# Second pieces of the first four attention units: the values' products from split parts in two passes, in place of float32

## The chip, the core and the metric

The kernel runs on one core of a Trainium2 chip. The engines are TensorE (PE in the profile, with its weight loads as PEld), VectorE (DVE), ScalarE (ACT), GpSimd (POOL) and SyncE (SP), which here issues every DMA. The metric is the device time in microseconds (us) of one execution, and a kernel's time is the median of its runs.

## The reference

Three layers follow one another, and every one takes and gives float32:

```python
# attention: B, H, S, D = 4, 8, 576, 64
scores = scale * q @ k^T ; causal mask ; a = softmax(scores)
local  = a @ v                                   # the products that the change touches
mem    = (phi(q) @ M_prev) / (phi(q) @ z_prev + 1e-6)
x      = g * mem + (1 - g) * local               # as 2304 x 512
# first layer: 512 -> 2048 -> 512, silu;  second layer: 512 -> 1024 -> 512, softmax times h, layer norm
```

## The kernel before

**Units.** The 32 pairs of batch and head are worked off as 16 units of two heads each, so four units make one batch. The first four units (`u < NN`, `NN = 4`) are cut into a first piece (queries 0 to 256) and a second piece (queries 256 to 576); units 4 to 15 are done whole. Each such piece is a *turn*; sorted by place, the first pieces are turns 0 to 3, the second pieces turns 4 to 7.

**A turn** runs over tiles of 128 queries. For one tile, TensorE makes the scores (`pss`), VectorE adds the mask and takes the maximum (`a`, `nm`), ScalarE takes the exponential, TensorE transposes the result in blocks of 128 (`pst`), and the blocks are copied out of PSUM into a wide tile `aT` (`t_hi`, `t_lo`). When all tiles of a head are there, `av` multiplies the values with `aT` (`psav`) and the sum goes into `xs`. `finish` scales it and adds the memory term into `X` on GpSimd.

**Two ways to multiply.** For the units below `NN` the values `rawv` and the tile `aT` are float32, and a product is one call, which shows in the trace as two matmul records. The tiles `aTh` and `aTl` are then two buffers of that one kind, and turns take them by turns (`turn_of[u] % 2`); the values alternate too, between the buffers `rawv` and `vhl`. For the other units everything is split in two parts that TensorE takes in one pass each: `aTh` is the rounded part (made by ScalarE) and `aTl` the rest (a subtraction on VectorE), `vhl` holds the rounded values (a cast on VectorE) beside their rest (a subtraction on GpSimd); a product is then two matmuls into one accumulator, one with `aTh` and one with `aTl`, and both halves of the accumulator are added (a copy on ScalarE and an addition on VectorE).

**The fill.** Between the turns TensorE works on the first layer of batches whose `X` is ready (`psh`, `psfy`). While the second pieces run there is only the fill of batch 0, columns 0 to 256: 72 matmuls `psh` and 72 `psfy`. The next, columns 256 to 576, needs all four second pieces. The weights `w` for it are split once on the way (`wraw` to `wf` to `w`), three VectorE instructions for each half chunk.

**The order** is not that of the source. Every call gets a due time (`call`, `at`), and a planner (`Order.plan`) goes through a model of the five engines: it takes the operation that can start first, then the one due first, as far as buffers are free, and writes the operations down in that sequence. Each engine then works its own queue in order. Nearly all instructions are issued by one line of this class, which the profile calls L360, so tiles' names tell them apart.

The lines that decide which way a unit goes:

```python
n = ("f", turn_of[u] % 2) if u < NN else ("r", n)                       # a_of
if u < NN: v_t[u] = raw.rearrange("p c j d -> p c (j d)"); return        # split_v, cut
for to, ps in t_pairs(u, t) if u >= NN else ():                          # t_lo
```

Of the kernel before, what the change touches and what calls it, by code (L numbers as in the profile page):

```python
# [11 lines left out]
F32 = mybir.dt.float32  # L12
F32R = mybir.dt.float32r
# [22 lines left out]
NN = 4  # L36
# [327 lines left out]
def body(ctx, tc, qk, qk2, qt, vp, mz, beta, w1, w2i, w2o, gln, out):  # L364
# [150 lines left out]
    st = {}  # L515
    heads, raws, v_t, mem_t, s_t, unit, X, Xd, Yd = {}, {}, {}, {}, {}, {}, {}, {}, {}
    a_t = {}

    def a_of(u, n=0):


        n = ("f", turn_of[u] % 2) if u < NN else ("r", n)
        if n not in a_t:
            a_t[n] = p1.tile([128, 3840], F32 if u < NN else F32R, tag=f"aT{n[1]}", name="aT" + "hl"[n[1]])

            act.copy(heads_of(a_t[n])[64:128, :, 1024:1088], tri[64:128, 0:128].rearrange("p (j q) -> p j q", j=2))
        return a_t[n]


# [46 lines left out]

    def load_v(u, q1):
        n = (q1 + 127) // 128
        st["v"] = st.get("v", 0) + (u < NN)
        raws["v", u] = p1.tile([128, 5, 2, 64], F32, tag="vhl" if u < NN and st["v"] % 2 else "rawv", name="rawv")[:, 0:n]  # L580
        sp.dma_start(raws["v", u], vp[u, :, 0:n].rearrange("p c (j d) -> p c j d", j=2))

    def split_v(u, q1):
        raw = raws.pop(("v", u))
        if u < NN:
            v_t[u] = raw.rearrange("p c j d -> p c (j d)")
            return
        vhl = p1.tile([128, 5, 2, 128], F32R, tag="vhl", name="vhl")[:, 0:(q1 + 127) // 128]
        dve.tensor_copy(vhl[:, :, :, 0:64], raw)
        pool.tensor_tensor(vhl[:, :, :, 64:128], raw, f32(vhl[:, :, :, 0:64]), ALU.subtract)  # L590
        v_t[u] = vhl
# [155 lines left out]
    def heads_of(w):  # L747
        return w[:, 0:3840].rearrange("p (j c) -> p j c", j=2)
# [20 lines left out]
    def t_hi(u, t, n):  # L769
        turn_of[u] = n  # L770
        for to, ps in t_pairs(u, t):
            if u < NN and t > 4:
                dve.tensor_copy(to(a_of(u)), ps)
            else:
                act.copy(to(a_of(u)), ps)

    def t_lo(u, t):
        for to, ps in t_pairs(u, t) if u >= NN else ():
            dve.tensor_tensor(to(a_of(u, 1)), ps, f32(to(a_of(u))), ALU.subtract)
        s_t.pop((u, t))  # L780

    def av(u, j, segs, last):
        vhl = v_t[u]
        if ("s", u) not in unit:
            unit["s", u] = p2.tile([128, S], F32, tag="xs", name="xs")
        xs = unit["s", u]
        to, other = (UP, LOW) if j == 0 else (LOW, UP)
        for q0, q1 in segs:
            ps = ps_a.tile([128, q1 - q0], F32, tag="av", name="psav")
            kbs = [kb for kb in range(5) if 128 * kb < q1]  # L790
            for kb in kbs:
                f = max(q0, 128 * kb)
                w = a_cols(j, kb, f, q1)
                if u < NN:
                    pe.matmul(ps[:, f - q0:], vhl[:, kb], a_of(u)[:, w], start=(kb == 0), stop=(kb == kbs[-1]))
                    continue
                pe.matmul(ps[:, f - q0:], vhl[:, kb, j, :], a_of(u)[:, w], start=(kb == 0), stop=False)
                pe.matmul(ps[:, f - q0:], vhl[:, kb, j, :], a_of(u, 1)[:, w], start=False, stop=(kb == kbs[-1]))
            if u < NN:
                act.copy(xs[to, q0:q1], ps[to])  # L800
                continue
            act.copy(xs[to, q0:q1], ps[other])
            dve.tensor_tensor(xs[to, q0:q1], ps[to], xs[to, q0:q1], ALU.add)
        if last:
            v_t.pop(u)
# [365 lines left out]
```

## Time and profile before

| | before |
|---|---|
| three runs | 925.24, 929.64, 929.32 us |
| median | 929.32 us |
| the profiled execution: its own time | 926.01 us |
| its span, first to last instruction | 923.2 us |
| PE busy | 880.5 us (95%) |
| DVE busy | 593.7 us (64%) |
| ACT busy | 495.8 us (54%) |
| POOL busy | 401.8 us (44%) |

The profiled execution took 926.01 us, of which 2.8 us lie around the span; it is 3.3 us below the median. Busy time is the union of an engine's instructions, and matmul ends are modelled, so neighbouring matmuls overlap in the rows: how long a row of them takes is read from start to start, not from the durations. Starts are counted from the begin of the span.

### The profile page before, as it was taken

What the parts mean: (1) busy time and instruction counts of PE and PEld (TensorE: products, weight loads), DVE (VectorE), ACT (ScalarE), POOL (GpSimd) and SP (SyncE); (2) the same over time, 40 slices, a digit from 0 to 9 for tenths busy, and PEclk for the clock granted to TensorE, in tenths of its full rate; (3) what the DMA queues carried; (4) which work ended last, traced back from release to release, by engine and by line L of the source; (5) the groups of instructions that cost most, each with busy time, mean ns of one, the idle gap of its engine ahead of it and who ended that gap; (6) DMA issues with size and microseconds to landing.
All of it is one profiled execution on the core that took longest, in us unless ns stands there. A gap on an engine that the chain in (4) does not pass through costs nothing.

```text
span 923.2 us, 15757 instructions
## 1 busy us (share of the span) xinstructions
PE 880.5 (95%) x5762; PEld 801.8 (87%) x5762; DVE 593.7 (64%) x1396; ACT 495.8 (54%) x1201; POOL 401.8 (44%) x334
## 2 busy tenths in 40 slices
PE   8989999999999999999889998899899999999998
PEld 6666899998899999998889998799889888888886
DVE  4777779878777757157984228832656666666663
ACT  5767689878787867455553335434443333232222
POOL 4555588877767653334542225423533111111110
PEclk9999999999999999999999999999999999999999
DMA  6525243343323210453342003300000000000000
GB/s 214 167 86 174 89 158 109 123 142 100 108 88 102 89 42 1 184 227 124 115 136 92 1 1 114 111 5 1 1 1 2 12 23 23 24 23 24 23 24 34
DMA packets 26653, 71.97 MB, mean 78 GB/s; under 512 B 3152, under 2 KB 10064, under 8 KB 25680
## 3 DMA queue, kind: packets, MB, share of 16 engines
q1 hardware_dynamic: 26576, 70.97, 23.3%
q8 instruction: 45, 0.74, 0.3%
q14 instruction: 32, 0.26, 0.1%
HBM read 60.34 MB, written 10.62 MB: 77 GB/s over the span
## 4 chain that ended last, share of the span: by engine, by line
PE 68%; DVE 18%; ACT 6%; issue 4%; DMA 3%; POOL 0%; ACTq 0%; DVEq 0%; SPq 0%
PE psh L360 24%; PE pso L360 11%; PE psy L360 11%; DVE wf L360 9%; PE pst L360 5%; PE psav L360 5%; PE pss L360 5%; PE psfy L360 5%; DMA wraw<-in_w 2%; DVE phe L360 2%; DVE a L360 1%; DVE aTl L360 1%; PE psr L360 1%; ACT wf L360 1%; PE psm L360 1%
## 5 line engine op out<-in xcount | busy, mean ns | idle before, releaser
L360 PE MATMUL psh<-xh,w 128*128 128x288 f32 (+2 forms) x1024 | 205.4, 300 | 1.7 <-ACT w L360 1.7
L360 PEld LDWEIGHTS psh<-xh,w 128*128 128x128 f32 x1024 | 161.5, 189 | 4.0 <-ACT w L360 1.9
L360 POOL TENSOR_TENSOR xl<-x,xh 128x1152 fp32r<-128x1152 f32 (+3 forms) x35 | 88.1, 2520 | 117.7 <-ACT xh L360 108.1
L360 PE MATMUL psh<-xl,w 128*128 128x288 f32 (+2 forms) x512 | 137.2, 299 | 0.0
L360 DVE TENSOR_TENSOR glo<-psh,gh 128x288 fp32r<-128x288 f32 (+2 forms) x128 | 57.7, 452 | 120.3 <-ACT gh L360 120.2
L360 PE MATMUL psy<-gh,w 128*128 128x288 f32 x736 | 117.1, 297 | 7.4 <-DVE y L360 4.1
L360 PEld LDWEIGHTS psy<-gh,w 128*128 128x128 f32 x736 | 104.2, 188 | 10.5 <-ACT gh L360 5.4
L360 POOL TENSOR_TENSOR w<-wf,w 128x512 fp32r<-128x512 f32 x48 | 65.8, 1372 | 103.4 <-ACT w L360 103.3
L360 PE MATMUL pso<-w,tb 128*128 128x512 f32 x432 | 104.0, 397 | 0.0
L360 ACT ACTIVATE a<-a,nm 128x128 f32<-128x128 f32 (+4 forms) x144 | 84.5, 588 | 23.2 <-DVE nm L360 21.9
L360 PEld LDWEIGHTS pso<-w,tb 128*128 128x128 f32 x432 | 79.9, 188 | 17.2
L360 PEld LDWEIGHTS psh<-xl,w 128*128 128x128 f32 x512 | 91.7, 190 | 0.1
L360 PE MATMUL psh<-w,yh 128*128 128x512 f32 x288 | 90.2, 394 | 0.0
L360 DVE SCALAR_TENSOR_TENSOR wf<-wraw,wf 128x512 uint32<-128x512 uint32 x96 | 86.7, 903 | 3.1
L360 DVE CUSTOM_DVE_ANT_0 a<-pss,tri 128x128 f32<-128x128 f32 (+4 forms) x144 | 67.6, 476 | 21.3 <-PE pss L360 17.4
L360 PE MATMUL psy<-glo,w 128*128 128x288 f32 x368 | 68.3, 301 | 12.2 <-DVE glo L360 12.1
L360 PE MATMUL pst<-ident,a 128*128 128x128 f32 (+1 forms) x400 | 70.2, 280 | 5.0 <-ACT rb L360 2.1
L360 ACT ACTIVATE psh<-psh 128x288 f32<-128x288 f32 x84 | 33.1, 395 | 72.0 <-PE psh L360 71.9
L360 DVE TENSOR_TENSOR aTl<-pst,aTh 128x128 fp32r<-128x128 f32 (+3 forms) x120 | 56.2, 484 | 18.6 <-ACT aTh L360 18.2
L360 PEld LDWEIGHTS psy<-glo,w 128*128 128x128 f32 x368 | 55.5, 191 | 14.0 <-DVE glo L360 14.0
L360 PE MATMUL psfy<-gh,w 128*128 128x288 f32 (+2 forms) x288 | 63.6, 303 | 1.8 <-ACT w L360 1.7
L360 PEld LDWEIGHTS psh<-w,yh 128*128 128x128 f32 x288 | 53.9, 188 | 11.9
(129 smaller groups left out, 1900.3 us busy)
## 6 DMA issues: line engine op xcount, KB each, us to landing
wraw<-in_w SPq DMA_DIRECT2D x32, 512.0 KB, 3.8
rawqk<-in_qk SPq DMA_DIRECT2D x24, 608.0 KB, 3.9
rawv<-in_vp SPq DMA_DIRECT2D x16, 320.0 KB, 3.1
out<-ob SPq DMA_DIRECT2D x18, 256.0 KB, 2.0
wraw<-in_w2i SPq DMA_DIRECT2D x8, 512.0 KB, 3.6
wraw<-in_w2o SPq DMA_DIRECT2D x8, 512.0 KB, 3.6
rawq<-in_qt SPq DMA_DIRECT2D x12, 288.0 KB, 2.8
y<-yd SPq DMA_DIRECT2D x3, 1152.0 KB, 14.4
```

Of the source, the lines that this page charges most:

```text
L360: getattr(target, method)(*[real(a) for a in args], **{k: real(v) for k, v in kw.items()})
```

## The change

A new function `whole(u)` takes the place of `u < NN` where values and `aT` are concerned. It is true in turns 0 to 3 only, the first pieces. So the second pieces (turns 4 to 7) now take the split way: `aTh` and `aTl` are the two parts of one tile, the values are loaded into `rawv` and split into `vhl`, and the products are two one-pass matmuls each. Scores, norms and the memory term of these units stay in float32. Due times and tables are unchanged.

```diff
+    def whole(u):
+        return turn_of[u] < NP
...
-        n = ("f", turn_of[u] % 2) if u < NN else ("r", n)
+        n = ("f", turn_of[u] % 2) if whole(u) else ("r", n)
...
-            a_t[n] = p1.tile([128, 3840], F32 if u < NN else F32R, tag=f"aT{n[1]}", name="aT" + "hl"[n[1]])
-            act.copy(heads_of(a_t[n])[64:128, :, 1024:1088], tri[64:128, 0:128].rearrange("p (j q) -> p j q", j=2))
+            a_t[n] = p1.tile([128, 3840], F32 if whole(u) else F32R, tag=f"aT{n[1]}", name="aT" + "hl"[n[1]])
+            if not whole(u):
+                act.copy(heads_of(a_t[n])[64:128, :, 1024:1088], tri[64:128, 0:128].rearrange("p (j q) -> p j q", j=2))
...
-        st["v"] = st.get("v", 0) + (u < NN)
-        raws["v", u] = p1.tile([128, 5, 2, 64], F32, tag="vhl" if u < NN and st["v"] % 2 else "rawv", name="rawv")[:, 0:n]
+        st["v"] = st.get("v", 0) + (q1 < S)
+        raws["v", u] = p1.tile([128, 5, 2, 64], F32, tag="vhl" if q1 < S and st["v"] % 2 else "rawv", name="rawv")[:, 0:n]
...
-        if u < NN:
+        if q1 < S:
             v_t[u] = raw.rearrange("p c j d -> p c (j d)")
...
-            if u < NN and t > 4:
+            if whole(u) and t > 4:
                 dve.tensor_copy(to(a_of(u)), ps)
...
-        for to, ps in t_pairs(u, t) if u >= NN else ():
+        for to, ps in t_pairs(u, t) if not whole(u) else ():
             dve.tensor_tensor(to(a_of(u, 1)), ps, f32(to(a_of(u))), ALU.subtract)
...
-                if u < NN:
+                if whole(u):
                     pe.matmul(ps[:, f - q0:], vhl[:, kb], a_of(u)[:, w], start=(kb == 0), stop=(kb == kbs[-1]))
...
-            if u < NN:
+            if whole(u):
                 act.copy(xs[to, q0:q1], ps[to])
```

The planner lays the whole program out anew. TensorE, the values' products of turn 4 (the unit's two heads, one accumulator `psav` each), as they stood before:

```order
L360 MATMUL pss_777<-rawqk_327 128x512
L360 MATMUL psav_782<-aTh_120,rawv_510 128x320 x3
L360 MATMUL psav_782<-aTh_120,rawv_510 128x192
L360 MATMUL psav_782<-aTh_120,rawv_510 128x64
L360 MATMUL psav_799<-aTh_120,rawv_510 128x320 x3
L360 MATMUL psav_799<-aTh_120,rawv_510 128x192
L360 MATMUL psav_799<-aTh_120,rawv_510 128x64
L360 MATMUL psr_815<-ident_58,bc_725 128x128 x2
```

The same place now (the first head to its end, and the second head's first products):

```order
L360 MATMUL pss_786<-rawqk_325 128x288
L360 MATMUL psav_792<-aTh_513,vhl_641 128x320
L360 MATMUL psav_794<-aTh_513,vhl_641 128x320
L360 MATMUL pss_799<-rawqk_325 128x288
L360 MATMUL psr_805<-ident_58,bc_748 128x128
L360 MATMUL psav_792<-aTl_618,vhl_641 128x320
...
L360 MATMUL psav_792<-aTh_513,vhl_641 128x192
L360 MATMUL psav_792<-aTl_618,vhl_641 128x192
L360 MATMUL psav_792<-aTh_513,vhl_641 128x64
L360 MATMUL psav_792<-aTl_618,vhl_641 128x64
L360 MATMUL psav_794<-aTl_618,vhl_641 128x320
```

Five float32 products a head became five pairs; the first product with `aTh` of both heads goes ahead, and the first with `aTl` stands behind it in the same queue.

VectorE before, from the end of turn 4's scores (`a,nm` is the maximum, `wf` a weight's split, `phe` and `rn` belong to the memory term, `psh` to the fill):

```order
L360 COPY aTh<-pst 128x3x128
L360 ISA a,nm<-pss,trip,nm 128x288
L360 ISA nm 128x1
L360 TENSOR_SCALAR wf<-wf 128x512
L360 SCALAR_TENSOR_TENSOR wf<-wraw,wf 128x512 x2
L360 SCALAR_TENSOR_TENSOR phe<-rawq,phe 128x320
L360 RECIPROCAL sums<-sums 128x5
```

And now:

```order
L360 TENSOR_TENSOR aTl<-pst,aTh 128x3x128
L360 ISA a,nm<-pss,trip,nm 128x288
L360 ISA nm 128x1
L360 TENSOR_SCALAR wf<-wf 128x512
L360 SCALAR_TENSOR_TENSOR wf<-wraw,wf 128x512 x2
L360 CAST vhl<-rawv 128x10x64
L360 SCALAR_TENSOR_TENSOR phe<-rawq,phe 128x320
L360 TENSOR_TENSOR aTl<-pst,aTh 128x3x128
L360 RECIPROCAL sums<-sums 128x5
```

The copy of a tile became a subtraction, the subtraction of the other head's tile and the cast of the values came into the queue, and what stood behind them moved back by as much.

## Rows read from the trace of the kernel before

**Rows 1.** The profile's busy times, and its chain that ended last, by engine.

```profile
PE 880.5 (95%) x5762; PEld 801.8 (87%) x5762; DVE 593.7 (64%) x1396; ACT 495.8 (54%) x1201; POOL 401.8 (44%) x334
PE 68%; DVE 18%; ACT 6%; issue 4%; DMA 3%; POOL 0%; ACTq 0%; DVEq 0%; SPq 0%
```

**Rows 2.** Busy time by stretch: stretch: length, busy us (instructions) by engine, clock, DMA.

```profile
41.00:119.00 78.00, 70.40 (x424) 54.50 (x423) 56.61 (x133) 53.27 (x135) 45.39 (x46) 1.00 0.42 135
119.00:372.00 253.00, 247.68 (x1876) 238.60 (x1875) 194.33 (x573) 204.08 (x547) 181.43 (x151) 1.00 0.29 92
372.00:383.00 11.00, 10.91 (x80) 10.48 (x80) 0.46 (x1) 4.29 (x8) 4.52 (x6) 1.00 0.22 65
383.00:923.00 540.00, 515.06 (x3197) 471.31 (x3196) 318.16 (x600) 208.32 (x436) 151.84 (x99) 0.99 0.16 55
```

**Rows 3.** TensorE's timeline, 40 to 120: its longest idle times, in brackets.

```profile
52.49 0.98 PE L360 MATMUL pst<-ident,a 128*128 128x128 f32 x7 [1.38 <-ACT aTh L360]
68.46 1.12 PE L360 MATMUL pss<-rawqk 64*128 64x512 f32 x2 [1.36 <-DVE nm L360]
83.96 1.09 PE L360 MATMUL pst<-ident,a 128*128 128x128 f32 x8 [1.66 <-ACT rb L360]
106.48 0.38 PE L360 MATMUL psfy<-gh,w 128*128 128x256 f32 x1 [1.72 <-ACT w L360]
```

**Rows 4.** The chain in order of time: start, us, what; two second pieces' products.

```profile
54.88 4.47 PE psav L360 x20
89.21 4.27 PE psav L360 x20
```

**Rows 5.** TensorE's timeline, a later unit's split products of one head.

```profile
299.88 0.42 PE L360 MATMUL psav<-aTl,vhl 128*128 128x320 f32 x1
300.13 0.31 PE L360 MATMUL psav<-aTh,vhl 128*128 128x320 f32 x1
300.28 0.31 PE L360 MATMUL psav<-aTl,vhl 128*128 128x320 f32 x1
...
301.08 0.66 PE L360 MATMUL psr<-ident,bc 128*128 128x128 f32 x4
```

**Rows 6.** Groups by shape, whole span: xcount | busy us, mean ns | idle before.

```profile
L360 DVE TENSOR_TENSOR aTl<-pst,aTh 128x512 fp32r<-128x512 f32 x36 | 24.8, 688 | 10.9 <-ACT aTh L360 10.7
L360 DVE TENSOR_TENSOR aTl<-pst,aTh 128x384 fp32r<-128x384 f32 x24 | 13.1, 548 | 0.0
L360 DVE TENSOR_TENSOR aTl<-pst,aTh 64x128 fp32r<-64x128 f32 x12 | 3.3, 276 | 0.7 <-ACT aTh L360 0.7
L360 DVE CAST vhl<-rawv 128x640 fp32r<-128x640 f32 x12 | 7.3, 608 | 2.5 <-PE psav L360 2.5
L360 DVE TENSOR_TENSOR xs<-psav,xs 64x320 f32<-64x320 f32 x24 | 11.7, 487 | 5.2 <-ACT xs L360 4.8
L360 DVE COPY aTl<-pst 128x512 f32<-128x512 f32 x2 | 1.4, 685 | 0.0
L360 DVE COPY aTl<-pst 128x384 f32<-128x384 f32 x2 | 1.1, 548 | 0.0
L360 ACT CAST aTh<-pst 128x512 fp32r<-128x512 f32 x36 | 21.0, 582 | 1.1 <-PE pst L360 0.9
L360 ACT CAST aTh<-pst 128x384 fp32r<-128x384 f32 x24 | 11.6, 481 | 2.5 <-PE pst L360 2.3
L360 POOL TENSOR_TENSOR vhl<-rawv,vhl 128x640 fp32r<-128x640 f32 x12 | 20.0, 1668 | 15.6 <-DVE vhl L360 15.6
```

**Rows 7.** As rows 2, three later stretches of units done the split way.

```profile
119.00:140.00 21.00, 20.51 (x156) 19.34 (x156) 16.83 (x53) 19.06 (x51) 18.65 (x15) 1.00 0.38 120
140.00:160.00 20.00, 19.55 (x147) 18.41 (x146) 19.16 (x57) 19.07 (x55) 16.54 (x15) 1.00 0.40 124
160.00:180.00 20.00, 19.76 (x150) 18.88 (x149) 17.09 (x52) 17.68 (x47) 17.37 (x16) 1.00 0.34 104
```

**Rows 8.** TensorE's waits, 119 to 372: total us, times, longest.

```profile
PE psav L360 <- DVE aTl L360: 1.2, 3, 0.8
```

**Rows 9.** Timelines of VectorE and GpSimd, around 115: a cast beside a product.

```profile
114.77 1.58 DVE L360 CAST vhl<-rawv 128x640 fp32r<-128x640 f32 x1
114.75 1.25 POOL L360 TENSOR_TENSOR bc<-rn,g 128x640 f32<-128x640 f32 x1
```

## The prediction, as it went on record

> **What bounds the kernel now.** The first look goes to the busy times and to the chain that ended last [rows 1]: TensorE is busy for 95% of the span and is 68% of the chain, VectorE is 18% of it. TensorE's work is therefore the first thing to count, and the next question is whether that holds in the stretch that the change touches. The table by stretch answers it [rows 2]. The second pieces of the first four units lie between 41 and 119 us: the first products of turn 4 start at 54.88 [rows 4], and fill of the next kind comes only after the fourth piece. There TensorE is busy 70.4 of 78 us, so 7.6 us idle, VectorE 56.6, ScalarE 53.3, GpSimd 45.4. This is the only stretch before the end of attention in which TensorE has idle time worth the name: from 119 to 372 it is busy 247.7 of 253, and from 372 to 383, when attention is over, it works off left-over fill at 10.9 of 11. The four long idle times in the stretch are in the timeline [rows 3]: 1.38 for a copy of a tile out of PSUM, 1.36 for a maximum, 1.66 and 1.72 for ScalarE, which had a row's sums or a weight to copy. So the stretch is TensorE's first, and where it is not, it waits for the chain of VectorE and ScalarE.
>
> **The change part by part.** *TensorE.* One second piece's products are 20 records; from the first to the next kind of work they took 4.47 and 4.27 us in the two that went through without a break [rows 4], call it 4.35. The later units make the same shapes in the split way, ten matmuls for a head. In one of them the eight from 300.13 to the next kind of work at 301.08 took 0.95 us, and a 320-column one costs 0.15 from start to start (300.13 to 300.28), so ten take 0.95 + 2 x 0.15 = 1.25; in that row the first one with `aTl` took 0.25 instead of 0.15 before the next could start, which makes 1.35 [rows 5]. A unit has two heads: 2.5 to 2.7 us. The saving is 4.35 - 2.6 = 1.75 us for a unit, 7.0 us for the four (6.6 to 7.4 by those ends).
>
> *VectorE.* A second piece has tiles of 384, 512, 384, 512 and one of 512 with 64 x 128. Each now gets a subtraction: 3 x 0.688 + 2 x 0.548 + 0.276 = 3.44 us. To that come the cast of the values, 0.608, and two additions to `xs`, 2 x 0.487 = 0.97. Two copies leave, 0.685 + 0.548 = 1.23, since ScalarE takes them over [rows 6]. Net 5.02 - 1.23 = 3.79 us for a unit, 15.2 us for the four, and this lies wholly in the stretch.
>
> *ScalarE* gains those two tiles, 0.582 + 0.481 = 1.06 us for a unit, 4.3 in all. *GpSimd* gains the rest of the values, 4 x 1.668 = 6.7 us [rows 6]. Both come out with room in the stretch: ScalarE 53.3 + 4.3 = 57.6, GpSimd 45.4 + 6.7 = 52.1 of 78 us.
>
> *The sum for the stretch.* TensorE 70.4 - 7.0 = 63.4 us, VectorE 56.6 + 15.2 = 71.8 us. That turns the two round. TensorE alone, with its old idle time, would let the stretch shrink to 71 us; VectorE cannot do its work in less than 71.8, and needs more as far as it idles. How dense can it be? The nearest rows are the three stretches just behind, where units are done the split way [rows 7]: VectorE is busy 19.16 of 20 us in one, which is 0.958, and 16.83 + 19.16 + 17.09 = 53.08 of 61 in all three, which is 0.870, with TensorE over 0.97 busy in every one. At 0.958 the stretch takes 71.8 / 0.958 = 74.9 us, a gain of 3.1; at 0.870 it takes 82.5, a loss of 4.5. I take the upper value. In the three rows together TensorE was the fuller engine, so VectorE had to idle there, while here it would be the fuller one; and the products that it now waits behind are shorter. The lower value stays as the far end.
>
> *Further on.* A gain at 119 us reaches the end whole: TensorE is the bound from there to 383 [rows 2], and nothing later starts by the clock. If the attention units come late out of the stretch, TensorE has fill to do meanwhile, because 10.9 us of it were left after attention anyway [rows 2]; that cover hides a VectorE that lags behind after 119, not one before it, since fill of the second kind needs all four pieces.
>
> *New waits.* `aTh` and `aTl` are now one pair for all second pieces, where two turns alternated before. A turn's first copy therefore waits for the products of the turn before. And in TensorE's queue the first product with `aTl` stands with all that is behind it, scores and transposes of the next turn, until VectorE has subtracted the last tile. The later units live with both: TensorE waited for `aTl` at that place 1.2 us in all, three times, 0.8 at the longest [rows 8], among the 24 heads of twelve units. For eight heads that is 0.4 us by the mean and 6.4 by the longest; I take 0.4, because the order puts the `aTh` products and some scores ahead of it just as there, and because it lies inside the time in which VectorE is the bound. The values' load must now wait until the cast has emptied `rawv`; the cast follows the products of the turn before, and a turn lasts 78 / 4 = 19.5 us, so it costs nothing unless the cast itself is late.
>
> *The pair of VectorE and GpSimd.* One row shows a cast of the values that took 1.58 us, where the mean is 0.608; a GpSimd product had begun 0.02 us before it and lasted 1.25 [rows 6, 9]. The means of rows 6 contain such meetings at the rate of the later units, so the sum has no further term for them. The Trainium skill states it as a rule that speaks against this change ("SBUF — State Buffer", section "Who interferes with whom"): a VectorE cast in its two-port mode, or an operation with two SBUF inputs, and a GpSimd instruction exclude each other for a whole instruction. The trace's 1.58 us agrees with it. By that rule alone each of the four new GpSimd subtractions could hold VectorE once for its full length, 6.7 us more, and the stretch would be (71.8 + 6.7) / 0.958 = 81.9 us, a loss of 3.9.
>
> **The rivals.** *VectorE takes over in part (the forecast)*: the stretch goes from 78 to 74.9; 3 us are gained. In the profile's own time 926.0 becomes 923.0; the profiled run lies 3.3 us under the median, and from the median 929.3 the forecast is **926.3 us**.
>
> *All of it comes through*: 7.0 us, 922.3. Speaks for it: the planner fills TensorE well, 97.9% from 119 on, and a VectorE that is behind at 119 does no harm later. Speaks against: it needs VectorE full throughout and part of its work moved out past 119, and the order keeps the work of the next units' memory term ahead of turn 7's additions.
>
> *Nothing comes through*: TensorE's freed 7 us turn into idle time in front of the same VectorE and ScalarE waits as in rows 3; 929.3, give or take 1. This is VectorE at 71.8 / 78 = 0.92 busy.
>
> *Slower*: VectorE gets no denser than the 0.870 of the three later stretches. The point from which this decides is 0.92; below it the stretch grows, at 0.870 by 4.5 us, which gives 933.8. The place is the end of each turn, where the last subtraction holds the first `aTl` product and with it the next turn's scores, which VectorE needs to go on. The rule on the shared pair leads to the same side, by 3.9 us: 933.2. Its chance is counted in here, and is small, since the later units carry twelve such GpSimd subtractions in rows where VectorE reached 0.958.
>
> *The change does not do what it says* (planned orders differ everywhere, and the stretches behind 119 could lose or gain a few us by chance): TensorE has 5.3 us of idle time from 119 to 372, so a loss or gain beyond 2 us from this is unlikely; I widen the range by that much.
>
> **How the numbers follow.** Chances: partial gain 0.43, whole gain 0.27, nothing 0.17, slower 0.13. About 0.5% (4.6 us) is what a measurement of this kernel can tell from no change. Faster by more than that needs nearly the whole gain: 0.24 of the 0.27, and 0.07 of the partial gain, 0.31. Slower by more than that is the far half of the slow case and its chance additions, 0.10. The rest, 0.59, lies within. The range leaves about a tenth on either side: the whole gain with 2 us of chance, 920.0, and the slow case short of its end, 932.5.
>
> **What would show it.** In the profile after, the products of a second piece must be 20 matmuls in about 2.6 us, and VectorE's sum over the stretch must rise by about 15 us. Right: the stretch from the first second-piece score to the first fill of columns 256 to 576 is some 3 us shorter, VectorE is over 0.93 busy in it, TensorE's idle time there rises from 7.6 to about 11.5 us, and its waits name `aTl`, `nm` or ScalarE behind VectorE. Wrong towards faster: TensorE's idle time stays near 7.6. Wrong towards slower: VectorE stays under 0.92, with waits of 0.5 us and more for `aTl` at most of the eight heads. If the stretch gains 3 us and the end does not, the loss lies behind 119 and the sum of this text has missed it.

## The result, and the profile after

Over six runs each, in the same rounds, the changed kernel takes 933.77 us (933.08 to 935.36) and the kernel before 926.33 us (925.24 to 929.64): a ratio of 1.0083, with a 95% interval of 1.0061 to 1.0105. The change makes the kernel slower by 0.6 to 1.05%, where 3 us of gain were forecast. The profiled execution of the changed kernel took 933.78 us, that of the kernel before 926.01.

The page after, its busy times and its chain by engine, to be read beside [rows 1]:

```profile
span 932.0 us, 15814 instructions
PE 883.7 (95%) x5768; PEld 806.1 (86%) x5768; DVE 611.8 (66%) x1424; ACT 500.8 (54%) x1207; POOL 409.5 (44%) x338
PE 68%; DVE 19%; ACT 6%; issue 4%; DMA 2%; POOL 0%; ACTq 0%; DVEq 0%; SPq 0%; POOLq 0%
```

The shares hardly move: 18.1 us more of VectorE is the only large figure, and it is still idle for a third of the span. The table by stretch, after, with the first two cuts of [rows 2], tells more:

```profile
41.00:119.00 78.00, 64.59 (x394) 50.59 (x392) 69.45 (x152) 54.08 (x134) 47.50 (x45) 0.96 0.39 121
119.00:372.00 253.00, 246.32 (x1852) 236.60 (x1852) 195.96 (x570) 201.85 (x536) 182.90 (x150) 0.99 0.31 97
```

In the stretch of the second pieces TensorE has done 30 instructions fewer by 119 us and is idle 13.4 us instead of 7.6; VectorE is busy 69.5 of 78 us. Behind 119 TensorE is nearly as full as it was, 246.3 of 253 us. The same work ends later: the first `psh` of the next fill starts at 130.26 us, before at 123.49. From 240 us on everything is late by 7.6 to 7.9 us (the 360th fill matmul starts at 241.32 instead of 233.44), and apart from some 35 us around 460, where the two kernels' clocks fall at different places, it stays so up to 654. There 0.9 us come on top: the changed kernel is granted 0.50 from 661.1 to 664.5, the kernel before is not at that place. Cut so that both hold nearly the same work, up to that `psh`, the table reads, before and then after (the second holds 25 TensorE instructions and some 2 us of VectorE work of later units more):

```profile
41.00:123.50 82.50, 74.90 (x459) 58.68 (x458) 59.03 (x141) 57.73 (x147) 48.93 (x48) 1.00 0.44 139
```

```profile
41.00:130.30 89.30, 75.78 (x484) 61.52 (x482) 76.28 (x174) 62.76 (x155) 56.79 (x51) 0.96 0.41 132
```

VectorE has 17.3 us more to do and is busy 0.854 of the longer stretch. The last column but two is the granted clock, and it is lower. TensorE's waits in these two stretches (engine and tile that waits, what ended it, us in total, times, longest), before and then after:

```profile
PE pst L360 <- ACT rb L360: 1.9, 2, 1.7
PE psfy L360 <- ACT w L360: 1.7, 1, 1.7
PE pss L360 <- DVE nm L360: 1.7, 2, 1.4
PE pst L360 <- ACT aTh L360: 1.4, 1, 1.4
```

```profile
PE psr L360 <- DVE aTl L360: 2.4, 1, 2.4
PE pst L360 <- ACT w L360: 2.4, 1, 2.4
PE psfy L360 <- ACT w L360: 2.3, 1, 2.3
PE pst L360 <- ACT rb L360: 2.2, 2, 1.5
PE pss L360 <- DVE nm L360: 1.8, 3, 0.9
```

**The new wait.** Until turn 6 nothing is lost: the products of turns 4, 5 and 6 start at 55.5, 71.3 and 89.2 us, before at 54.8, 72.4 and 89.0. Those of turn 7 start at 112.8 instead of 104.0, so the loss arises between the two. The longest wait there stands in turn 6. TensorE's timeline after (start, us, what, in brackets the idle time before it and what ended it):

```profile
89.24 0.56 PE L360 MATMUL psav<-aTh,vhl 128*128 128x320 f32 x2
92.83 0.30 PE L360 MATMUL psr<-ident,bc 128*128 128x128 f32 x1 [2.44 <-DVE aTl L360]
92.89 0.39 PE L360 MATMUL psav<-aTl,vhl 128*128 128x320 f32 x1
...
94.29 0.31 PE L360 MATMUL psav<-aTh,vhl 128*128 128x320 f32 x1
...
95.23 0.33 PE L360 MATMUL psr<-ident,bc 128*128 128x128 f32 x1
```

and VectorE's, and below it GpSimd's, at the same time:

```profile
88.37 1.16 DVE L360 TENSOR_SCALAR wf<-wf 128x512 uint32<-128x512 uint32 x1
89.57 2.52 DVE L360 SCALAR_TENSOR_TENSOR wf<-wraw,wf 128x512 uint32<-128x512 uint32 x2
92.00 0.68 DVE L360 TENSOR_TENSOR aTl<-pst,aTh 128x512 fp32r<-128x512 f32 x1
```

```profile
87.70 1.55 POOL L360 TENSOR_TENSOR st<-rawqk,st 64x640 fp32r<-64x640 f32 x1 [1.41 <-issue]
89.33 1.48 POOL L360 TENSOR_TENSOR kl<-rawqk,st 128x576 fp32r<-128x576 f32 x1
```

TensorE has two `aTh` products and then nothing, because the subtraction that makes `aTl` stands on VectorE behind the three steps of a weight. These took 3.7 us beside two GpSimd instructions; the same three took 1.84 us in the kernel before (0.42 + 1.42, from 87.66). The two GpSimd instructions are not new: in the kernel before, an `st` and a `kl` met another weight's three steps from 63.64, and those took 3.85 us (1.33 + 2.52). What is new is that a subtraction which TensorE waits for stands behind such a meeting. The step after that is the raw weights' one buffer: the next load is issued when VectorE's last step is done, at 92.53 instead of 89.63, then at 101.62 instead of 97.16, and the two waits for `w` above, 2.4 and 2.3 us, are its end.

**The lower clock.** The table by stretch after, around the end of turn 6, and once more at 197:

```profile
104.00:108.20 4.20, 2.27 (x15) 1.58 (x15) 3.41 (x5) 2.12 (x5) 4.04 (x4) 1.00 0.51 166
108.20:115.00 6.80, 5.21 (x21) 4.95 (x22) 5.38 (x15) 3.77 (x11) 2.33 (x4) 0.50 0.05 19
196.90:200.30 3.40, 3.40 (x16) 3.36 (x15) 2.31 (x9) 2.73 (x5) 3.05 (x4) 0.50 0.46 129
```

TensorE was busy 2.27 of 4.2 us at a granted 1.00 (2.4 GHz), and then it was granted 0.50 (1.2 GHz) for 6.8 us. The kernel before is granted 1.00 in both places, although its TensorE was hardly busier in the first one; its row there:

```profile
104.00:108.20 4.20, 2.48 (x12) 1.66 (x11) 4.03 (x8) 1.40 (x4) 1.74 (x4) 1.00 0.00 0
```

So the busy share ahead of the fall doesn't say alone why the clock fell. The timeline after shows the price in the products themselves, from start to start: 0.26 us from 114.71 to 114.97, 0.14 from 115.14 to 115.28.

```profile
114.71 0.45 PE L360 MATMUL psav<-aTh,vhl 128*128 128x320 f32 x1
114.97 0.33 PE L360 MATMUL psav<-aTl,vhl 128*128 128x320 f32 x1
115.14 0.30 PE L360 MATMUL psav<-aTh,vhl 128*128 128x320 f32 x1
115.28 0.31 PE L360 MATMUL psav<-aTl,vhl 128*128 128x320 f32 x1
```

**The balance.** The first 250 us, before and then after, give it in one row each:

```profile
0.00:250.00 250.00, 234.14 (x1571) 203.16 (x1571) 187.96 (x539) 190.13 (x508) 169.87 (x167) 1.00 0.43 134
```

```profile
0.00:250.00 250.00, 227.27 (x1522) 197.46 (x1523) 201.30 (x553) 190.56 (x503) 173.28 (x167) 0.98 0.41 130
```

TensorE is idle 250 - 227.27 = 22.7 us instead of 15.9, so 6.9 more. The 10.2 us at half clock cost at most half of it, 5.1. The kernel is 7.6 to 7.9 us behind by then. That less 6.9 and less 5.1 leaves -4.4 to -4.1 us for TensorE's own work: of the 7.0 us that were to be saved at most some 4 are visible, and idle time and clock take back up to 12.

### The profile page after: what moved, and what is told of

It is laid out like the page before. It is cut to its first block, busy times and chain, and to the rows that moved or that the text cites. A ratio compares the mean times of both kernels' runs of the same rounds, so it can differ in the third digit from the quotient of the medians.

```text
span 932.0 us, 15814 instructions
## 1 busy us (share of the span) xinstructions
PE 883.7 (95%) x5768; PEld 806.1 (86%) x5768; DVE 611.8 (66%) x1424; ACT 500.8 (54%) x1207; POOL 409.5 (44%) x338
## 4 chain that ended last, share of the span: by engine, by line
PE 68%; DVE 19%; ACT 6%; issue 4%; DMA 2%; POOL 0%; ACTq 0%; DVEq 0%; SPq 0%; POOLq 0%
PE psh L360 24%; PE psy L360 11%; PE pso L360 11%; DVE wf L360 10%; PE pst L360 5%; PE pss L360 5%; PE psfy L360 5%; PE psav L360 4%; DVE a L360 2%; DMA wraw<-in_w 2%; DVE aTl L360 2%; PE psr L360 1%; ACT wf L360 1%; DVE phe L360 1%; ACT a L360 1%
## 5 line engine op out<-in xcount | busy, mean ns | idle before, releaser
L360 PE MATMUL psy<-gh,w 128*128 128x288 f32 x736 | 119.1, 300 | 6.9 <-DVE y L360 4.8
L360 PE MATMUL pso<-w,tb 128*128 128x512 f32 x432 | 104.0, 397 | 0.0
L360 ACT ACTIVATE a<-a,nm 128x128 f32<-128x128 f32 (+4 forms) x144 | 84.4, 587 | 23.9 <-DVE nm L360 23.0
L360 PEld LDWEIGHTS pso<-w,tb 128*128 128x128 f32 x432 | 79.9, 188 | 17.1
L360 DVE TENSOR_TENSOR aTl<-pst,aTh 128x512 fp32r<-128x512 f32 (+4 forms) x144 | 69.5, 498 | 18.3 <-ACT aTh L360 17.5
L360 DVE CUSTOM_DVE_ANT_0 a<-pss,tri 128x128 f32<-128x128 f32 (+4 forms) x144 | 67.4, 476 | 18.8 <-PE pss L360 14.1
L360 PE MATMUL psfy<-gh,w 128*128 128x288 f32 (+2 forms) x288 | 66.1, 308 | 2.7 <-ACT w L360 2.3
L360 ACT CAST aTh<-pst 128x512 fp32r<-128x512 f32 (+4 forms) x144 | 59.8, 435 | 9.4 <-PE pst L360 8.2
## 6 DMA issues: line engine op xcount, KB each, us to landing
y<-yd SPq DMA_DIRECT2D x3, 1152.0 KB, 15.2
```

The lines of the kernel that those rows point to most:

```text
L360: getattr(target, method)(*[real(a) for a in args], **{k: real(v) for k, v in kw.items()})
```

## The experiments

Theories: VectorE's added work is what costs (A in the expectations; their B is the form of the products: one buffer for all turns, the cast, the queue's head); TensorE's saving has no worth in this stretch, whatever VectorE does; the weights' line (one raw buffer, VectorE's three steps, ScalarE's copy) is pushed back and fill comes late (C); the planner's new order as such costs, and not the work (D). Ratios are to the kernel before on the same chip in the same rounds, with 95% intervals. "Idle" and "clock" are TensorE's idle time and granted clock in the first 250 us.

| kernel | median us | ratio | idle | clock |
|---|---|---|---|---|
| changed kernel | 933.77 | 1.0083 (1.0061 to 1.0105) | 22.7 | 0.98 |
| high part alone | 927.41 | 1.0021 (1.0009 to 1.0032) | 18.3 | 0.96 |
| VectorE's work alone | 931.37 | 1.0058 (1.0041 to 1.0075) | 16.6 | 0.99 |
| turn 7 alone | 931.21 | 1.0053 (1.0033 to 1.0073) | 19.8 | 0.99 |
| turns 5 to 7 | 930.26 | 1.0045 (1.0029 to 1.0060) | 19.5 | 0.98 |
| two raw buffers, changed | 930.43 | 1.0049 (1.0034 to 1.0064) | 25.8 | 0.98 |
| two raw buffers, before | 929.82 | 1.0042 (1.0022 to 1.0062) | 16.6 | 0.97 |
| longer weights' line, before | 931.89 | 1.0063 (1.0043 to 1.0084) | 18.2 | 0.98 |
| useless products, changed | 931.56 | 1.0060 (1.0045 to 1.0075) | 17.8 | 0.99 |

**High part alone.** The changed kernel without the subtractions for `aTl` and the products with it in turns 4 to 7, so the lower part of these `aT` is left out of the result:

```
-        for to, ps in t_pairs(u, t) if not whole(u) else ():
+        for to, ps in t_pairs(u, t) if u >= NN else ():
...
+                if u >= NN:
                     pe.matmul(ps[:, f - q0:], vhl[:, kb, j, :], a_of(u, 1)[:, w], ...)
```

> The changed kernel, but in the second pieces the values' products take the high part alone: the subtractions for the low part aTl and their five matmuls a head are left out (so the low part is missing from the result), all else stays (one buffer for all turns, the values' cast, GpSimd's subtraction, the additions to xs). Removes 3.44 us of VectorE work a turn, 13.8 in all, and some 5 us of TensorE. Theory A (VectorE's added work sets the stretch from 41 to 119 us): the loss goes and the saving of TensorE comes through, 4 to 9 us faster than the kernel before, 917 to 922 us. Theory B (the form of the products: one buffer for all turns, the values that must be cast first, queue heads of TensorE): the loss of 7.4 us stays for the most part, 928 to 933 us.

It took 927.41 us. TensorE has still less to do than in the changed kernel and VectorE's heaviest addition is gone; the kernel is nonetheless not faster than before. The table by stretch of this kernel shows where the saving went:

```profile
61.30:71.50 10.20, 10.20 (x34) 6.49 (x34) 7.91 (x19) 5.49 (x14) 7.02 (x7) 0.50 0.32 101
102.20:105.60 3.40, 3.36 (x13) 3.25 (x13) 1.67 (x7) 2.22 (x7) 3.39 (x4) 0.50 0.48 154
112.50:119.30 6.80, 6.12 (x25) 5.28 (x25) 5.39 (x15) 4.49 (x13) 6.40 (x5) 0.50 0.28 96
```

20.4 us at half clock, which is up to 10.2 us lost, where the kernel before has none. The time is above what A expects and just under the range of its rival; neither had the clock in its numbers. So the saving does not come through even with most of VectorE's new work away; that it went into the clock is the reading that fits, not a separate test.

**VectorE's work alone.** The kernel before, with an idle subtraction of the same shape in PSUM after each tile of the second pieces, 24 instructions that add 13.8 us; TensorE's work and its products stay:

```
+            elif n >= NP:
+                dve.tensor_tensor(ps, ps, to(a_of(u)), ALU.subtract)
```

> The kernel before, with the subtractions alone added to the second pieces: after each copy of a tile VectorE subtracts it from the blocks in PSUM, in place, and nobody reads the result. TensorE's products stay float32, the buffers alternate as before. Adds 13.8 us of VectorE work to the stretch. Theory A: slower than the kernel before by 5 to 14 us, since nothing is saved in return, 931 to 940 us. Theory B: within 2 us of the kernel before, 924 to 929 us.

931.37 us, within A's range. With VectorE's work as the one addition the kernel costs 5.4 us more by the ratio; the planned order is another too, which the orders below show to be worth nearly as much. Its route is not quite that of the changed kernel: TensorE's idle time hardly grows (16.6 us), but TensorE is granted 0.50 once, early, and it is busy throughout that time:

```profile
47.40:54.20 6.80, 6.80 (x21) 4.12 (x20) 2.33 (x5) 2.26 (x7) 1.07 (x2) 0.50 0.20 62
```

The high part alone costs 0.21% and VectorE's work alone 0.58%; together 0.79%, and the whole change costs 0.83%. That the two add up so well must not be leaned on, given how much orders scatter (below).

**Turn 7 alone, and turns 5 to 7.** The split way for the last of the four turns, or for the last three (`5` in place of `7`):

```
-        return turn_of[u] < NP
+        return turn_of[u] < 7
```

> Only the fourth second piece (turn 7) takes the split way, turns 4 to 6 stay as before. Theory A by a quarter of VectorE's work: 1 to 3 us slower than before, 927 to 929 us. If instead the place decides (the loss shows in the trace between the products of turns 6 and 7, where the last weights of the fill come), turn 7 alone carries most of it: 4 to 8 us slower, 930 to 935 us.

> Turns 5, 6 and 7 take the split way, turn 4 stays as before. Theory A by three quarters of the work: 4 to 7 us slower than before, 930 to 934 us. If turn 7 decides, the same as with turn 7 alone.

931.21 and 930.26 us. One turn costs 4.9 us by the ratio, three 4.2, four 7.7: the cost does not grow turn by turn, and a quarter of VectorE's work costs more than A's 1 to 3 us. With turn 7 alone its products start at 108.6, 4.6 us late, while the three turns ahead keep time. Either the place in turn 7 decides or any new order costs some; these two kernels alone can't tell the one from the other.

**Two raw buffers, in the changed kernel and in the kernel before.** For the first stage, the half chunk of a weight is loaded as two pieces of 256 columns in two buffers, so that a load no longer waits for VectorE's last step (the same edit in both):

```
-            raw = temp.tile([128, 512, 2], U32, tag="wraw", name="wraw")
-            sp.dma_start(raw, src[:, n])
+            for h in range(2 if temp is p1 else 1):
+                raw = (p2 if temp is p1 else temp).tile([128, 256 if temp is p1 else 512, 2], U32, tag="wraw", name="wraw")
+                sp.dma_start(raw, src[:, n, cut])
```

> The changed kernel; in the first stage a weight's half chunk is loaded in two pieces of 256 columns into two raw buffers of half the size (same memory), so that the next load need not wait for VectorE's last step on the piece before. Theory C (the line of the twelve weight loads, each waiting for VectorE's work on the one before, sets the end of the stretch, and TensorE's saving falls into waiting for it): the last weight comes 10 us and more earlier than 109 us, TensorE's waits for w go, and the kernel gains 6 to 12 us on the changed kernel, 921 to 927 us; it is then faster than the kernel before with the same edit. Theory A (VectorE's sum sets the stretch): the edit adds some VectorE time, so no gain, 932 to 937 us.

> The kernel before with the same edit as e5. Theory C: a small gain or none, 0 to 4 us (921 to 926 us), since TensorE had 7.6 us of idle time there and one wait of 1.7 us for a weight; e5 lies below this run. Theory A: no gain, and e5 stays 5 to 8 us above this run.

930.43 and 929.82 us. The changed kernel's copies of `w` come earlier (the last begins at 104.47 instead of 109.12), and the waits for `w` are gone from its list, but TensorE waits for VectorE instead. Its waits from 41 to 130 us:

```profile
PE pss L360 <- DVE nm L360: 4.3, 5, 2.0
PE pst L360 <- DVE aTl L360: 4.1, 2, 3.4
PE psh L360 <- DVE glo L360: 3.6, 1, 3.6
```

The time lies in neither theory's range (921 to 927 by C, 932 to 937 by A), but C as the sole cause falls: with the weights out of the way VectorE is what TensorE waits for. The kernel before even loses 3.9 us by the edit, which breaks each of VectorE's steps in two, so the small gap between the two kernels of this pair (0.07%) is not the cost of the change in the usual order.

**A longer weights' line.** The kernel before, with the masking step of each first-stage weight done twice on VectorE:

```
+            if i < P0:
+                dve.tensor_scalar(f, f, 0, 0x7FFFFFF8, ALU.logical_shift_left, ALU.bitwise_and)
```

> The kernel before; VectorE's second step on each half chunk of a weight of the first stage is done twice (the second time changes nothing), which adds 0.43 to 0.7 us to each of the twelve, and nothing else changes. Adds 5 to 8 us of VectorE work, and as much to the line of weight loads. Theory C: the last weight comes 5 to 8 us later and the kernel is 3 to 7 us slower, 929 to 933 us, for less than half of the VectorE work that the change adds. Theory A: by VectorE's share, under 2.5 us slower, 925 to 928 us.

931.89 us, within C's range and above A's (925 to 928); the last copy of `w` begins at 112.2 instead of 105.8. It speaks for VectorE work in this line costing more than its share, but does not show it, nor that the line is how the change costs: the orders below move the kernel before nearly as far (5.3 of the 5.8 us).

**Useless products.** The changed kernel with two float32 products with zeros more for each accumulator of the second pieces, 8.5 us of TensorE work that adds nothing to the sums:

```
+                if u < NN and kb == 0:
+                    for _ in range(2):
+                        pe.matmul(ps, ident, tri[:, 0:q1 - q0], start=False, stop=False)
```

> The changed kernel with two float32 products of zeros added to each of the eight accumulators of the second pieces, behind the first product with aTh: 8 x 2 x 0.53 = 8.5 us of TensorE work that adds zero. If TensorE's time set the stretch it would cost 6 to 9 us, 940 to 943 us. By theory C it falls into waiting and costs 0 to 3 us, 934 to 937 us; and if the stretches at the lower clock (108 to 115 and 197 to 200 us in the changed kernel) come from TensorE's thinner work, they shrink, and the run is at or under the changed kernel, 930 to 934 us.

931.56 us, 1.0060 against the changed kernel's 1.0083: 8.5 us of TensorE work cost nothing. This is one kernel in one new order; but for a lucky order to hide the full price it would have to give back 8.5 + 2.1 us, and the five orders of the changed kernel below span 6.4 us. The first 250 us show where the work went:

```profile
0.00:250.00 250.00, 232.23 (x1560) 202.12 (x1560) 198.31 (x553) 190.51 (x503) 171.66 (x167) 0.99 0.41 131
```

Idle time falls from 22.7 to 17.8 us and the time at half clock from 10.2 to 3.4 (100.2 to 103.6). Together that is 4.9 + 3.4 = 8.3 us given back (the 3.4 at most), the work that was put in. This is the worthless saving from the other side: beside VectorE's new work up to 8 us of TensorE's work are free, so taking 7 us away could not bring much. What TensorE's work is worth in the kernel before was not tried in this way.

**Orders.** What stays is the order. Four changes of numbers that touch no work, each made in both kernels: the weights' due time by two steps, the place of batch 0's fill by two, the distance of the second pieces from 6 to 6.25, and the planner's estimate of the weights' three steps set near the measured times:

```
-       ... "fill": 6, "w": 3}
+       ... "fill": 6, "w": 5}
...
-FILL = [(0, 0, 256, 14, 38), ...
+FILL = [(0, 0, 256, 16, 40), ...
...
-T_Z = (3, 12, 6)
+T_Z = (3, 12, 6.25)
...
+        if outs and outs[0].buf.name == "wf":
+            return (720 if method == "tensor_scalar" else 900), 0
```

> The kernel before; the weights of the first stage are due 5 places after their turn in place of 3, and nothing else: the same instructions in another planned order. Theory D (the order before is the best of many tried on the chip, and any new order costs some us, whatever work it carries): 2 to 6 us slower, 928 to 932 us. If the loss of the changed kernel comes from its work and not from its order: within 1.5 us of before, 924 to 927 us.

> The kernel before; the first fill's places begin at 16 and end at 40 in place of 14 and 38, the same instructions in another order. Theory D: 2 to 6 us slower, 928 to 932 us. Else within 1.5 us of before, 924 to 927 us.

> The changed kernel with the weights due 5 places after their turn in place of 3. Theory D: the changed kernel is one draw of many, so this one may lie anywhere from 924 to 936 us, and its distance to e9 is under 4 us. If the work decides: 931 to 936 us, and 5 to 9 us above e9.

> The changed kernel with the first fill's places at 16 to 40 in place of 14 to 38. Theory D: anywhere from 924 to 936 us, under 4 us from e10. If the work decides: 931 to 936 us, and 5 to 9 us above e10.

> The kernel before; the second pieces' places are 6.25 apart in place of 6, the same instructions in another order. If any new order costs the clock and some waits, as in e9 and e10: 2 to 6 us slower than before, 927 to 931 us, with at least one stretch at the lower clock before 250 us.

> The changed kernel with the same places as e13. If the change's own work costs about 6 us whatever the order (VectorE's added work makes TensorE wait 7 us longer, less some of the 7 us saved, plus lower clock): 3 to 9 us over e13, 931 to 938 us, and TensorE's idle time up to 250 us is 21 to 25 us against 15 to 18 in e13. If the order alone decides: within 3 us of e13.

> The kernel before, where the planner is told longer times for VectorE's three steps on each half chunk of weights, 0.72 and 0.9 us as the trace has them in the mean, in place of 0.33 and 0.60. No instruction changes, only the order. If orders differ by luck: 2 to 6 us slower than before, 927 to 931 us.

> The changed kernel with the same longer times for the weights. If the loss comes from a plan that counts too little of VectorE's work in this stretch: TensorE's idle time up to 250 us falls from 22.7 to under 19 us and the run is within 2 us of e15. If VectorE's work costs whatever the plan knows of it: 3 to 9 us over e15, idle time 21 us and more.

| order | without the change | with it | cost, us |
|---|---|---|---|
| as it was | 1 | 1.0083 (1.0061 to 1.0105) | 7.7 |
| weights' due time | 1.0035 (1.0014 to 1.0056) | 1.0114 (1.0092 to 1.0137) | 7.3 |
| fill's place | 1.0057 (1.0033 to 1.0081) | 1.0095 (1.0060 to 1.0130) | 3.5 |
| second pieces' distance | 0.9969 (0.9952 to 0.9986) | 1.0085 (1.0060 to 1.0110) | 10.7 |
| weights' true times | 0.9998 (0.9984 to 1.0013) | 1.0045 (1.0031 to 1.0059) | 4.4 |

The last column is the difference of the two ratios times the time of the kernel before. An order moves the kernel by -2.9 to +5.3 us, so any single kernel of this study carries that much chance. But the change costs in all five orders, 3.5 to 10.7 us, 6.7 us in the mean: the order alone is not the cause, the change's own work costs. (The pair of 3.5 us is not clear of the noise by itself, and lies under the 4 us that D allowed; the kernels before with the first two of the four new orders came out as slow as D had it, those with the last two did not.) The first 250 us of the pair with the second pieces' distance repeat what the first pair shows: VectorE is busy 203.08 us with the change instead of 187.58 without it, TensorE idle 23.2 us instead of 14.5, and the granted clock 0.98 instead of 1.00. TensorE's waits in this pair from 41 us to the first `psh` of the next fill (124.3 and 129.8) name what makes it idle. These are the ones that end on VectorE, without the change and then with it:

```profile
PE pss L360 <- DVE nm L360: 2.4, 2, 1.4
```

```profile
PE pst L360 <- DVE aTl L360: 3.0, 2, 2.5
PE psr L360 <- DVE aTl L360: 2.4, 1, 2.4
PE pss L360 <- DVE nm L360: 1.8, 3, 0.9
PE psm L360 <- DVE xs L360: 0.9, 1, 0.9
```

The same reading for all five orders, each without the change and with it, in us (idle time and time at a granted 0.50 in the first 250 us; waits from 41 us to the first `psh` of the next fill; the first `psy` begins the stage behind attention):

| order | TensorE idle | at 0.50 | waits for VectorE | waits for ScalarE | first `psy` |
|---|---|---|---|---|---|
| as it was | 15.9, 22.7 | 0, 10.2 | 1.7, 5.6 | 5.3, 6.9 | 384.2, 391.8 |
| weights' due time | 17.6, 24.2 | 13.7, 20.5 | 1.9, 11.6 | 4.3, 0.7 | 388.8, 394.6 |
| fill's place | 16.8, 23.7 | 6.8, 10.2 | 3.2, 11.0 | 3.6, 1.5 | 389.6, 393.7 |
| second pieces' distance | 14.5, 23.2 | 0, 10.2 | 2.4, 8.1 | 3.2, 3.2 | 384.1, 392.1 |
| weights' true times | 18.8, 21.7 | 17.1, 23.9 | 3.0, 9.6 | 3.6, 1.7 | 392.4, 395.1 |

In every order TensorE waits 3.9 to 9.7 us longer for VectorE, and its idle time with the change is above that of every order without it. Its waits for ScalarE grow in one pair and fall or stay in four. So the change costs by VectorE's part of it, theory A, though not by VectorE's sum alone: the waits are for `aTl`, `nm` and `xs`, results that TensorE needs next. The time at half clock grows in every pair too, but orders without the change have up to 17.1 us of it, so it belongs to the order as well. Where attention ends, the change costs 2.7 to 8.0 us; the rest of the scatter arises behind it.

The kernel before with the second pieces' distance at 6.25 takes 922.96 us beside 925.86 and is the fastest kernel of this study, by 0.31% (0.14 to 0.48%). That had not been expected of it. It needs none of the change, and its gain lies behind 250 us: the 360th fill matmul starts at 233.40, as in the kernel before, and the first `pso` of the last stage at 719.8 instead of 721.8.

## Why the prediction was wrong, step by step

**What bounds the kernel: half right.** TensorE is the bound elsewhere, and the changed kernel's loss does reach the end: 6.8 us at the first `psh` of the next fill, some 7.6 from 240 on, 8.8 at the end. It need not in every order: the kernel before with the weights' true times is 8.2 us late at the first `psy` and only 1.6 at the end. In the stretch itself the 7.6 us of idle time were read as slack beside a TensorE bound. With the change's VectorE work in it, the useless products show that TensorE's work has no price there; that the two chains already took turns in the kernel before is argued, from its waits for `nm` and for ScalarE's copies.

**TensorE's saving: the size right, its worth wrong.** Split products take what was forecast: in turn 6 the eight from 94.29 to the next kind of work at 95.23 take 0.94 us, forecast 0.95; eighteen of the twenty took 2.34 us, 92.89 to 95.23, and with the two ahead some 2.6, as forecast. Of the 7.0 us at most some 4 show up in the balance. They were paid for with idle time and clock.

**VectorE's work: 2 us short, for no single reason.** 17.3 us in the stretch instead of 15.2. By groups in the two stretches, before and then after (mean ns behind the comma):

```profile
L360 DVE SCALAR_TENSOR_TENSOR wf<-wraw,wf 128x512 uint32<-128x512 uint32 x18 | 15.5, 860 | 0.6
L360 DVE TENSOR_SCALAR wf<-wf 128x512 uint32<-128x512 uint32 x9 | 6.5, 723 | 1.1 <-ACT wf L360 1.0
```

```profile
L360 DVE SCALAR_TENSOR_TENSOR wf<-wraw,wf 128x512 uint32<-128x512 uint32 x18 | 17.5, 973 | 0.6
L360 DVE TENSOR_SCALAR wf<-wf 128x512 uint32<-128x512 uint32 x9 | 5.5, 616 | 0.7 <-ACT wf L360 0.7
L360 DVE CAST vhl<-rawv 128x640 fp32r<-128x640 f32 x5 | 4.6, 923 | 0.2 <-PE psav L360 0.2
```

The weights' three steps together took 23.0 us after and 22.0 before, and the cast took 923 ns in the mean where the sum had 608. The later units' work that the cut takes in is as large as either. The step "the sum has no further term" for the pair of VectorE and GpSimd was wrong for the casts: two of the five took 1.57 us, with a GpSimd `w<-wf,w` running as they began, the others 0.49. The rule that the Trainium skill gives ("SBUF — State Buffer", section "Who interferes with whom") pointed the right way, but not at its price: the four casts of the second pieces took 4.1 us where the sum had 2.4, and the rule's term was 6.7.

**How dense VectorE gets: the step that failed.** The forecast took 0.958, the best of three later rows, and put the mean of 0.870 down to TensorE being the fuller engine there. It came to 0.854 (76.28 of 89.3 us). By the forecast's density the VectorE work of the stretch as it was forecast, 59.0 + 15.2 us, fits into 77.5 us; 89.3 were measured. The larger sum makes 2.1 of the 11.8 us between them (76.28 / 0.958 = 79.6), the density 9.7. In the four other orders VectorE comes to 0.83 to 0.92 in the same stretch, never to 0.958. The text's own slower rival, "VectorE gets no denser than the 0.870", with its tipping point at 0.92, had the mechanism, at a chance of 0.13. That its 933.8 us is the measured time to a tenth is luck: it is a loss of 4.5 us from a base of 929.3, and the measured loss is 7.4 from 926.3. Cut at 104, in the last turn, the stretch after shows where the density went:

```profile
41.00:104.00 63.00, 53.11 (x326) 40.06 (x325) 58.02 (x129) 45.38 (x111) 40.14 (x38) 1.00 0.41 130
104.00:130.30 26.30, 22.67 (x159) 21.46 (x159) 18.26 (x46) 17.38 (x44) 16.66 (x14) 0.87 0.41 138
```

Up to 104 VectorE is busy 0.92 of the time, and from 62 to 104 even 0.95, near the forecast. Behind 104 it is busy 0.69, and 6.0 of its 8.0 us of idle time there end on ScalarE, whose copies it needs (`phe`, `xs`, `aTh`, `wf`). The forecast spread VectorE's sum evenly over the whole stretch; it could not move into the end of it, where VectorE waits for the last turn's results as it did before (11.82 of 19.5 us from 104 to 123.5). That a ring in which each engine waits for the next does not run at the best density of one of them is argued from this, not shown by a run of its own. In the order with the second pieces' distance at 6.25 the loss falls at the same place (turn 6's products at 89.2 against 87.2, turn 7's at 112.1 against 103.5); in the order with the fill's place it is spread, 2.0 to 3.4 us at each of the four turns.

**The wait at the queue's head: mis-sized.** 0.4 us were put for the eight heads. It was 2.44 us at one of them, and little at the others, so neither the forecast's 0.4 nor "0.5 us and more at most of the eight heads" describes it. Over the five orders TensorE's waits for `aTl` in the stretch come to 1.7 to 6.8 us. The mean of [rows 8] came from units without weight steps ahead of the subtraction.

**The clock: left out.** [Rows 2] showed 1.00 in the stretch before, and the text had no term for a change of it. It cost up to 5.1 us here, up to 10.2 in the kernel with the high part alone. The Trainium skill has a line against idle gaps between bursts of matmuls, since the clock falls back after them ("TensorE: Matmul & The Clock Gate", section "Why this matters for your kernels"). The trace agrees only in part. Ahead of the fall at 108.2 TensorE was busy 2.27 of 4.2 us, but no single wait in the stretch was longer than 2.44 us, the kernel before was busy 2.48 of the same 4.2 us and kept 1.00, and ahead of the fall at 196.9 the changed kernel was busy 6.29 of 6.9 us. Even so, a change that makes TensorE idle more should have had a rival on the clock.

**The base.** The forecast went from the median of three runs, 929.3; more runs put it at 925.2 to 926.3, which is the profiled execution's own time. Against this base 3 us of gain would have been 923.

**Open.** Why the clock fell in just these places, and how much of the cost is idle time and how much is clock, varies with the order and can't be given as one number. That the kernel before with the weights' true times has a clock of 0.97 in the first 250 us and is no slower at the end doesn't make the clock free: its 360th fill matmul starts 8.5 us late, and 6.6 us of its lag are made up behind attention, where its order differs too. The 3 us or more between the saving forecast and the one in the balance are not traced. The weights' line was only tried with edits that bring a new order with them, so its share of the waits is argued from the timelines, not shown by a run. Nor was VectorE's sum taken apart, under several orders, from the new form of the products (one pair of tiles for all turns, the queue's head): VectorE's work alone, without that form, gave 6.5 us of waits for VectorE in the stretch to 132.1 where the kernel before has 1.7, in one order.

## What to carry to other kernels

Before costing a saving on the fullest engine, ask in the stretch itself whether that engine's work has a price: if it has idle time there, adding useless work of the same size tells (here 8.5 us cost nothing). Where the saving is bought with work of another engine, take the mean density of the rows in question, not the best of them, count the idle time that stands in these rows beside the busy time, and look what stands ahead of the new instruction in its queue. In a kernel whose order a planner makes, try a change under several orders before believing a difference of half a per cent: here orders alone gave -0.3 to +0.6%. What each pair has in common, here the longer waits for VectorE, is the change's own.

## What the runs showed of the hardware

Two-input VectorE steps on 128x512 words took 0.69 us in most cases, and up to 1.80 and 1.91 us in others. Their shortest, middle and longest time in ns, before and then after, from 41 us to the first `psh` of the next fill:

```profile
L360 DVE SCALAR_TENSOR_TENSOR wf<-wraw,wf x18: 691/693/1796, 41.8 to 105.1; 128x512 uint32<-128x512 uint32 x18
L360 DVE SCALAR_TENSOR_TENSOR wf<-wraw,wf x18: 691/693/1914, 41.2 to 107.3; 128x512 uint32<-128x512 uint32 x18
```

The six over 1 us after, and the four before, all ran beside a GpSimd `TENSOR_TENSOR`; the longest after began at 99.65, beside an `st` that ran from 99.14 to 101.01. Not every one beside GpSimd was long: before, the step at 95.12 took 0.69 us, with an `xs` that began after it at 95.42.

TensorE's clock fell to 0.50 not only after long idle times: in the changed kernel it was busy 6.29 of the 6.9 us ahead of the fall at 196.9, while the kernel before, busy 2.48 of the 4.2 us from 104.0, kept 1.00.
